# Two transformer blocks on cached keys and values: sums over the partitions as bf16 pairs, an earlier mean, a reordered end, and longer DRAM rows

## The chip, the cores and the metric

The kernel runs on one core of one Trainium2 chip. The metric is the device time of one execution in microseconds (us). The profiles call the engines PE (matrix products; PEld is its weight loads), DVE and ACT (vector and scalar work), POOL, and SP, which issues the loads. PSUM is the memory, in banks, that PE writes its results to. The kernel before takes 2348.97 us (median of 3 runs, 2348.39 to 2350.38).

## The reference, cut to what matters

One decode step for 8 batch rows: attention (32 heads of 128, 4096 cached keys and values, its own cache for every row and head) and a feed-forward network (FFN), run twice with the same caches and weights. I call the two passes layer 0 and layer 1.

```python
def _layernorm(x, axis=-1, eps=1e-5):
    m = jnp.mean(x, axis=axis, keepdims=True)
    v = jnp.var(x, axis=axis, keepdims=True)
    return (x - m) / jnp.sqrt(v + eps)
# A_x [8,1,640]; A_k_cache, A_v_cache [8,32,4096,128]; wq [640,4096]; wo [4096,640]; w1 [640,1728]; w2 [1728,640]
# _A_ref: q = x @ wq; softmax(q k^T / sqrt(128)) v for each row and head; then @ wo
# _B_ref: relu(x @ w1) @ w2
    x = A_x
    x = x + _A_ref(_layernorm(x, axis=-1), A_k_cache, A_v_cache, A_wq, A_wo)
    x = x + _B_ref(_layernorm(x, axis=-1), B_w1, B_w2)
    x = x + _A_ref(_layernorm(x, axis=-1), A_k_cache, A_v_cache, A_wq, A_wo)
    x = x + _B_ref(_layernorm(x, axis=-1), B_w1, B_w2)
    return x
```

The caches are 537 MB, and on-chip memory can't hold them, so most of them are read twice, once for each layer (988 MB in all).

## The kernel before

The kernel visits head pairs one by one: layer 0 of one batch row, then layer 1 of the same row, with two visits of the next row's layer 0 in between. Keys and values come in tiles of 512 KB into a ring of 26 buffers (the tile `arena`). At the end of a row's layer 0 comes what I call a **turn**: the output projection (`wo`), the FFN, and the first queries of layer 1, each needing the one before. In a turn 21 of the 26 buffers keep tiles that layer 1 will use again, so only five buffers pass the stream on, one 512 KB load each. Three more tiles are put aside ("stash") in five PSUM banks and a small tile.

```python
G = 26          # buffers of 512 KB
SPARE = 5       # of these, free for the stream in a turn
STASH = 3
...
    first = [(which, hp, g) for which, hp in first for g in range(UNIT)]
    keep = set(first[: G - SPARE])
    stash = first[G - SPARE : G - SPARE + STASH]
```

The chain of a turn (and of the end of layer 1, which handles all 8 rows at once):

```python
        for k in range(n_up):
            c += [own(15, "up", k)]
            if k == min(1, n_up - 1):
                c += [own(0, "var"), own(0, "root")]
        c += [own(0, "relu")] + [own(14, "down", k) for k in range(n_down)] + [own(0, "add")]
        if layer == 0:
            c += [own(2, "mean"), own(0, "center")] + query(b, 0)
            c += [own(1, "var2"), own(0, "root2")] + query(b, 1)
```

Sums over the 128 partitions are matmuls with a matrix of ones, in fp32. In `do_w` the sum of the residual row is added to the sum of the last head pair's output, which four matmuls with the column sums of `wo` give ahead of time:

```python
        def var():
            nc.tensor.matmul(var_ps[:, :nb], lhsT=ones_f, rhs=st.pop("s2"), start=True, stop=True)
        def relu():                                    # relu and the norm's factor in one operation
                    nc.vector.scalar_tensor_tensor(
                        out=hT[:rows, fs], in0=h[:rows, fs], scalar=0.0,
                        in1=_free(st["rstd"][:rows], [(0, fs.stop - fs.start), (1, nb)]), op0=ALU.max, op1=ALU.mult,
                    )
        def mean():
            nc.tensor.matmul(mean_ps[:, :1], lhsT=ones_f, rhs=st.pop("s1"), start=True, stop=True)
...
    def do_w(i):
        ...                                            # 10 matmuls with wo
        if "sums" in st:
            st["sum"] = sum_ps[:, :nb]
            nc.tensor.matmul(st["sum"], lhsT=ones_f, rhs=st.pop("sums"), start=True, stop=False)
            for n in range(4):
                nc.tensor.matmul(st["sum"], lhsT=_free(wo_sum[...], [(0, P)]), rhs=..., start=False, stop=(n == 3))
```

The stash is copied back by two engines in turn, from one PSUM tile each:

```python
    stash = [ps.tile([P, 2 * BANK], BF16, name=f"stash{n}_ps") for n in range(STASH * per - 1)]
    stash.append(sm.tile([P, 2 * BANK], BF16, name="annex", bufs=1))
...
            copy = nc.vector.tensor_copy if n % 2 else nc.scalar.copy
            copy(out=arena[:, u * GW + n * 2 * BANK : u * GW + (n + 1) * 2 * BANK], in_=t)
```

In DRAM each of the 128 partitions has a row of 32 pieces of 8192 bf16 numbers (the keys or the values of a head pair): exactly 512 KiB.

## Time and profile before

| | before |
|---|---|
| time, median | 2348.97 us |
| DMA engines busy on the load queue | 99.2% of the span |
| bytes through that queue | 988.12 MB |
| PE busy | 1406.6 us, 60% |
| last cache tile landed (its semaphore, in the trace) | 2334.10 us |
| from there to the end | 13.9 us |
| 4 KiB packets slower than usual (over 164 ns, usual 159) | 1030 of 27904 |

From the page of the profile, lines of its parts 1, 2, 3 and 6. Part 2 has 40 equal slices of the span (59 us each); DMA is the busy share in tenths and GB/s what the engines moved.

```profile
span 2348.0 us, 42121 instructions
DMA  9999999999999999999999999999999999999997
GB/s 410 431 432 399 432 431 432 432 404 434 431 433 426 408 434 433 432 425 417 431 430 434 420 415 432 432 433 413 414 430 433 431 409 421 433 430 431 391 432 308
q1 hardware_dynamic: 75412, 988.12, 99.2%
arena<-in_A_kv_dram SPq DMA_DIRECT2D x218, 512.0 KB, 6.1
```

The engines are busy in every slice, but they don't move equally much. Slices at 431 to 434 GB/s are calm; the eight dips (399, 404, 408 and so on) are the eight turns. The slope from 4 KiB packets (159 ns) to 32 KiB packets (1213 ns) is 435 GB/s, which agrees with the ceiling of 435 GB/s that the Trainium skill gives (DMA: Bandwidth & Descriptors, "Where 436 GB/s comes from"). The same section says that loads from DRAM are held to a lower limit of about 358 GB/s; here they run at 431 to 434, so the measurement decides. So two things can be shortened: what comes after the last landing, and the turns. The last line is the view of loads: 218 loads of 512 KB, the size that the turns use, with a median of 6.1 us from issue to landing.

The windows view of before, one calm stretch and two in turns. Columns: stretch and its length in us, busy us (and count) of PE, PEld (the weight loads of PE), DVE, ACT and POOL, granted clock, DMA share, GB/s.

```profile
960.00:980.00 20.00, 10.62 (x108) 3.43 (x108) 3.58 (x14) 2.89 (x6) 0.39 (x2) 0.50 1.01 433
1640.00:1660.00 20.00, 15.76 (x296) 10.33 (x291) 4.00 (x23) 4.23 (x16) 2.54 (x12) 0.50 1.00 368
2200.00:2220.00 20.00, 17.03 (x356) 11.19 (x357) 5.53 (x27) 6.17 (x18) 2.54 (x12) 0.50 0.93 360
```

The timeline of before, a part of the turn at 1644 us, with lines left out (start, length, engine, line, operation, out<-in, count, and in brackets the idle time before it and what ended it):

```profile
1644.38 0.60 PE L527 MATMUL small_ps<-hT,w_sb 128*128 128x1 bf16 x14 [0.32 <-DVE lsum L721]
1644.91 0.60 PE L621 MATMUL o_ps<-arena,P_sb 128*4 128x512 bf16 x4
1645.44 0.59 PE L540 MATMUL small_ps<-s_16759,few 128*128 128x1 f32 x2
1646.06 0.17 DVE L544 SCALAR_TENSOR_TENSOR xc<-small_ps,xT 128x5 f32<-128x5 f32 x1 [0.69 <-PE small_ps L540]
1646.28 0.25 PE L734 MATMUL small_ps<-few,o_sb 100*128 100x2 bf16 x4 [0.25 <-DVE xc L544]
1646.45 0.60 PE L621 MATMUL o_ps<-arena,P_sb 128*4 128x512 bf16 x4
1646.61 0.15 DVE L744 TENSOR_TENSOR oT<-small_ps,invL 128x2 bf16<-128x2 f32 x1
1647.66 0.41 PE L751 MATMUL small_ps<-oT,wo_sb 128*128 128x1 bf16 x10 [0.25 <-ACT qo L605]
1647.99 0.60 PE L621 MATMUL o_ps<-arena,P_sb 128*4 128x512 bf16 x4
1648.52 0.59 PE L507 MATMUL small_ps<-s_16773,few 128*128 128x1 f32 x2
1649.04 0.59 PE L621 MATMUL o_ps<-arena,P_sb 128*4 128x512 bf16 x4
```

L527 is the last part of the FFN's second product ("down"), L540 the fp32 mean (two instructions, 0.59 us), L507 the fp32 sum of squares for the queries, L621 are value tiles of the stream, L734 and L751 belong to the next row's attention output. A buffer comes free with each L621; they start at 1644.91, 1646.45, 1647.99 and 1649.04.

The timeline of before, the end, with lines left out:

```profile
2335.62 0.27 PE L734 MATMUL small_ps<-few,o_sb 100*128 100x2 bf16 x4 [0.75 <-ACT o_sb L729]
2336.14 0.41 PE L751 MATMUL small_ps<-qo,wo_sb 128*128 128x8 bf16 x10 [0.25 <-DVE qo L744]
2336.41 0.57 PE L757 MATMUL small_ps<-arena,few 128*128 128x8 f32 x2
2337.94 0.95 PE L501 MATMUL small_ps<-arena,w_sb 128*128 128x8 bf16 x30 [0.85 <-DVE xT L485]
2339.68 1.44 PE L501 MATMUL small_ps<-arena,w_sb 128*128 128x8 bf16 x40 [0.36 <-ACT arena L435]
2341.82 2.92 PE L527 MATMUL small_ps<-arena,w_sb 128*128 128x8 bf16 x70 [0.71 <-DVE arena L520]
2345.03 0.29 PE L782 MATMUL small_ps<-ident,ends 128*40 128x128 bf16 x1 [0.29 <-DVE ends L534]
```

The last value matmul ends at 2334.87 us. From it to the `wo` product (L751, "W") 1.27 us pass, from W to "up" (L501) 1.80, from up's start to down's end (L527) 6.80, and from there to the output's matmul (L782) 0.29.

### The profile page before, as it was taken

How to read it: one execution, taken by the hardware profiler on the slowest of the kernel's cores; microseconds unless marked ns; L12 is line 12 of the kernel's file. 1: busy time of each engine (PE TensorE's matmuls, PEld its weight loads, DVE VectorE, ACT ScalarE, POOL GpSimd, SP SyncE). 2: the span in 40 equal slices, each digit the busy share in tenths (PEclk: the TensorE clock that was granted, in tenths of full speed). 3: DMA queues.
4: the chain of work that ended last, by engine and by line, in shares of the span. 5: the costliest groups of instructions: out<-in, count | busy, mean ns of one | idle time of the engine just before them, and what ended most of it. 6: DMA issues, size and time to landing. Idle time of an engine off the chain costs nothing.

```text
span 2348.0 us, 42121 instructions
## 1 busy us (share of the span) xinstructions
PE 1406.6 (60%) x18352; PEld 593.5 (25%) x18352; DVE 477.1 (20%) x1928; ACT 430.0 (18%) x995; POOL 59.5 (3%) x296
## 2 busy tenths in 40 slices
PE   3547655585555855558545685556754577545856
PEld 1214211151112511125111341113311133111523
DVE  1113211121112211122111221112211122112212
ACT  1111211121111221112111121111211112111211
POOL 0000000000000000000000000000000000000000
PEclk9999955555555555555555555555555555555555
DMA  9999999999999999999999999999999999999997
GB/s 410 431 432 399 432 431 432 432 404 434 431 433 426 408 434 433 432 425 417 431 430 434 420 415 432 432 433 413 414 430 433 431 409 421 433 430 431 391 432 308
DMA packets 75597, 990.81 MB, mean 422 GB/s; under 512 B 8468, under 2 KB 8468, under 8 KB 36372
## 3 DMA queue, kind: packets, MB, share of 16 engines
q1 hardware_dynamic: 75412, 988.12, 99.2%
q8 instruction: 143, 2.34, 0.4%
q14 instruction: 42, 0.34, 0.0%
HBM read 988.08 MB, written 0.01 MB: 421 GB/s over the span
## 4 chain that ended last, share of the span: by engine, by line
DMA 70%; PE 20%; ACT 5%; DVE 3%; issue 1%; SPq 0%; DVEq 0%; ACTq 0%; POOL 0%; POOLq 0%
DMA arena<-in_A_kv_dram 70%; PE o_ps L621 5%; PE s_ps L639 4%; PE s_ps L629 4%; ACT P_row L689 2%; PE small_ps L597 1%; ACT P_sb L695 1%; ACT o_sb L729 1%; PE small_ps L734 1%; DVE mrow L647 1%; PE small_ps L501 1%; PE small_ps L702 1%; PE small_ps L751 1%; ACT nmax L687 1%; ACT nmax L691 1%
## 5 line engine op out<-in xcount | busy, mean ns | idle before, releaser
L621 PE MATMUL o_ps<-arena,P_sb 128*4 128x512 bf16 x4096 | 597.3, 595 | 420.4 <-DMA arena<-in_A_kv_dram 418.1
L629 PE MATMUL s_ps<-arena,qz 128*4 128x512 bf16 x3040 | 408.4, 598 | 259.6 <-DMA arena<-in_A_kv_dram 248.9
L621 PEld LDWEIGHTS <-P_sb 128*4 128x4 bf16 x4096 | 111.4, 88 | 548.8 <-issue 532.6
L647 DVE TENSOR_REDUCE mrow<-s_ps 100x1 bf16<-100x512 f32 x190 | 131.9, 694 | 355.2 <-PE s_ps L629 355.2
L729 ACT CAST o_sb<-o_ps 100x512 bf16<-100x512 f32 x256 | 150.0, 586 | 272.7 <-PE o_ps L621 270.7
L687 ACT ACTIVATE nmax<-small_ps 100x1 f32<-100x1 f32 x106 | 18.1, 171 | 800.8 <-PE small_ps L676 800.8
L639 PE MATMUL s_ps<-qo,arena 128*128 128x1 bf16 x4224 | 141.1, 165 | 33.0 <-DMA arena<-in_A_kv_dram 16.4
L639 PEld LDWEIGHTS <-arena 128*128 128x128 bf16 x4224 | 130.0, 104 | 45.4 <-DMA arena<-in_A_kv_dram 27.7
L629 PEld LDWEIGHTS <-qz 128*4 128x4 bf16 x3040 | 61.9, 84 | 309.2 <-issue 291.2
L709 DVE CAST P_sb<-small_ps 128x64 bf16<-128x64 f32 x190 | 42.6, 224 | 474.4 <-PE small_ps L702 474.4
L702 PE MATMUL small_ps<-few,P_row 100*128 100x16 bf16 x760 | 52.4, 179 | 96.8 <-ACT P_row L689 96.8
L687 ACT ACTIVATE nmax<-small_ps,q_scale 100x1 f32<-100x1 f32 x84 | 22.0, 261 | 418.5 <-PE small_ps L676 418.5
L721 DVE TENSOR_REDUCE lsum<-small_ps 128x2 f32<-128x64 f32 x256 | 57.4, 224 | 168.4 <-PE small_ps L715 168.4
L661 DVE TENSOR_REDUCE diag<-small_ps 1x2 bf16<-1x16 f32 x190 | 30.8, 162 | 280.6 <-PE small_ps L654 273.5
L702 PEld LDWEIGHTS <-P_row 100*128 100x128 bf16 x760 | 35.1, 107 | 191.7 <-ACT P_row L689 186.9
L734 PEld LDWEIGHTS <-o_sb 100*128 100x128 bf16 x1024 | 49.6, 108 | 108.7 <-ACT o_sb L729 77.4
L734 PE MATMUL small_ps<-few,o_sb 100*128 100x2 bf16 x1024 | 67.4, 170 | 11.4 <-DVE xc L544 1.8
L689 ACT ACTIVATE P_row<-s_ps,nmax 100x512 bf16<-100x512 f32 x106 | 72.8, 687 | 3.4
L597 PE MATMUL small_ps<-xq,wq_sb 128*128 128x1 bf16 x1280 | 52.0, 165 | 32.1 <-DVE qo L744 26.3
L654 PE MATMUL small_ps<-few,mrow 100*1 100x16 bf16 x190 | 35.7, 188 | 55.3 <-DVE mrow L647 55.3
L689 ACT ACTIVATE P_row<-s_ps,nmax,q_scale 100x512 bf16<-100x512 f32 x84 | 65.4, 778 | 2.8
L597 PEld LDWEIGHTS <-wq_sb 128*128 128x128 bf16 x1280 | 52.8, 104 | 45.3 <-issue 44.5
(205 smaller groups left out, 859.7 us busy)
## 6 DMA issues: line engine op xcount, KB each, us to landing
arena<-in_A_kv_dram SPq DMA_DIRECT2D x126, 4096.0 KB, 23.1
arena<-in_A_kv_dram SPq DMA_DIRECT2D x89, 2048.0 KB, 21.2
arena<-in_A_kv_dram SPq DMA_DIRECT2D x218, 512.0 KB, 6.1
arena<-in_A_kv_dram SPq DMA_DIRECT2D x16, 3072.0 KB, 22.0
arena<-in_A_kv_dram SPq DMA_DIRECT2D x38, 1024.0 KB, 10.4
arena<-in_A_kv_dram SPq DMA_DIRECT2D x10, 2560.0 KB, 19.9
arena<-in_A_kv_dram SPq DMA_DIRECT2D x15, 1536.0 KB, 20.4
wq_sb<-in_A_wq_dram SPq DMA_DIRECT2D x4, 1280.0 KB, 17.7
```

Of the source, the lines that this page charges most:

```text
L597: nc.tensor.matmul(q_ps[:, h : h + 1], lhsT=wq_sb[:, g, c, (2 * n + h) * Dh : (2 * n + h + 1) * Dh], rhs=xlns[b][:, 0, c : c + 1], start=( ...
L621: nc.tensor.matmul(o_ps[32 * c : 32 * c + CJ, :], lhsT=P_tiles[i][:, h, j : j + CJ], rhs=arena[:, at + c * CJ * Dh : at + (c + 1) * CJ * D ...
L629: nc.tensor.matmul(s_ps[32 * c : 32 * c + CJ, :], lhsT=qz[:, i % 3, c // 2, 3 - g : 3 - g + CJ], rhs=arena[:, at + c * BANK : at + (c + 1) ...
L639: nc.tensor.matmul(s_tiles[i][:, j : j + 1], lhsT=arena[:, at + n * P : at + (n + 1) * P], rhs=qo[:, b, h : h + 1], start=True, stop=True,)
L647: nc.vector.tensor_reduce(out=m_tiles[i][:OR, :1], in_=s_ps[:OR], axis=AX.X, op=ALU.max)
L687: nc.scalar.activation(out=nm[:OR, :1], in_=max_ps[:OR, :1], func=ACT.Copy, scale=less)
L689: nc.scalar.activation(out=P_rows[i][:OR], in_=s_ps[:OR], func=ACT.Exp, bias=nm[:OR, :1], scale=more)
L702: nc.tensor.matmul(P_ps[:, k * 4 * CJ : (k + 1) * 4 * CJ], lhsT=P_row[:OR, k * P : (k + 1) * P], rhs=rsel[:OR], start=True, stop=True,)
L709: nc.vector.tensor_copy(out=P_tiles[i].rearrange("p h (c k) -> p h c k", k=BANK // P), in_=P_ps.rearrange("p (k h c) -> p h c k", k=BANK / ...
L721: nc.vector.tensor_reduce(out=L, in_=lsum_ps.rearrange("p (h j) -> p h j", h=2), axis=AX.X, op=ALU.add)
L729: nc.scalar.copy(out=o_tiles[i][:OR], in_=o_ps[:OR, :].rearrange("p (j d) -> p j d", j=CJ))
L734: nc.tensor.matmul(oy[i][:, :2], lhsT=o_tiles[i][:OR, j, :], rhs=gsel[:OR, j, :], start=(j == 0), stop=(j == CJ - 1))
```

## The change

The change wants to shorten the turns and the end.

- **Longer rows:** each partition's DRAM row gets 4 KiB more, so that the rows don't start 512 KiB apart.
- **The layer-0 part (turns):** each fp32 sum becomes two bf16 matmuls (the rounded value and the rest, made by two DVE operations). The mean of the residual row is taken off one visit earlier. The norm's factor is multiplied in after the FFN instead of at the relu.
- **The end part:** the same for layer 1; besides, the four value tiles of the last head pair are used as weights, so that their result needs no gathering; the sum comes before W; the FFN runs in pieces, with up in two PSUM banks by turns and down in five. For that, the five stash tiles become one tile, and the temporaries of the start and the end move from a buffer of the ring to the small stash tile (`annex`).

The diff, cut to its core:

```diff
+PAD = 2048
...
+        if layer:
+            for k in range(n_up):
+                c += [own(15, "down", k)] + [own(0, "var"), own(0, "root")] * (k == n_up // 2)
+            return c + [own(0, "add")]
...
             if last_of[layer, b] == i and (layer == 0 or b == B - 1):
-                chains[-1] += [(0, ("S", i)), (16, ("W", i)), (0, ("YC", i))] + finish(layer, b)
+                chains[-1] += [(14, ("W", i)), (0, ("YC", i))] + finish(layer, b)
             elif layer == 0 or b == B - 1:
                 chains[-1] += [(10, ("W", i)), (0, ("Y", i))]
+                if last_of[layer, b] == next(v for v in range(i + 1, NV) if visits[v][:2] == (layer, b)):
+                    chains[-1] += [(0, ("S", i)), (2, ("SM", i)), (0, ("SC", i))]
...
-    stash = [ps.tile([P, 2 * BANK], BF16, name=f"stash{n}_ps") for n in range(STASH * per - 1)]
+    stash_ps = ps.tile([P, (STASH * per - 1) * 2 * BANK], BF16, name="stash_ps")
+    stash = [stash_ps[:, n * 2 * BANK : (n + 1) * 2 * BANK] for n in range(STASH * per - 1)] + [annex]
...
+    def halves(s, name):
+        t = temp([P, s.shape[1], 2], BF16, name)
+        nc.vector.tensor_copy(out=t[:, :, 0], in_=s)
+        nc.vector.tensor_tensor(out=t[:, :, 1], in0=s, in1=t[:, :, 0], op=ALU.subtract)
+        return t
+
+    def over_partitions(out, t):
+        for k in range(2):
+            nc.tensor.matmul(out, lhsT=ones_p, rhs=t[:, :, k], start=(k == 0), stop=(k == 1))
...
         def var():
-            nc.tensor.matmul(var_ps[:, :nb], lhsT=ones_f, rhs=st.pop("s2"), start=True, stop=True)
+            over_partitions(var_ps[:, :nb], st.pop("s2"))
...
+                for n in range(CJ) if i == len(visits) - 1 else ():   # last V tile as weights
+                    nc.tensor.matmul(
+                        (s_ps if h else o_ps)[:, :1], lhsT=arena[:, at + (c * CJ + n) * Dh : at + (c * CJ + n + 1) * Dh],
+                        rhs=P_tiles[i][:, h, j + n : j + n + 1], start=(j + n == 0), stop=(j + n == NJ - 1),
+                    )
...
-    kv = kv.reshape(B, p, -1)
+    kv = np.pad(kv.reshape(B, p, -1), ((0, 0), (0, 0), (0, PAD)))
```

## The prediction

> **What bounds it now.** DMA. The page has the 16 DMA engines 99.2% busy on the load queue and 988 MB in 2348.0 us. Steady stretches of the windows view run at 424 to 441 GB/s. By the DMA packets of the trace, a 32 KiB packet takes 1213 ns and a 4 KiB one 159 ns, as do 90% of each size; the slope is 435 GB/s, the fabric ceiling that the Trainium skill gives (DMA: Bandwidth & Descriptors, "Where 436 GB/s comes from"). What can move:
>
> 1. The tail. The last load's wait ends at 2331.8 us (timeline), 16.3 us before the end.
> 2. Eight turns from layer 0 to layer 1, one for each batch row: windows there show 360 to 415 GB/s and PE 80 to 88% busy. 21 of 26 buffers are kept there, the rest filled by 512 KB loads (218, landing after 6.1 us), and buffers come free only as PE's chain moves. Packets over their minimum sum to 20 us of DMA time, some 15 in the turns. In the worst stretch (1646 to 1655 us, about 310 GB/s) PE takes some 1.5 us per tile against 1.25 for a load: I read this as underfed DMA.
>
> **Costs of the change.**
> - Partition sums: an fp32 matmul takes 0.56 to 0.59 us; two bf16 ones should take about 0.15 (four of the same form take 0.26). Three or four per turn: 1.2 to 1.7 us less PE. Each adds two DVE operations of 0.15 us.
> - Norm factor behind the FFN: relu waited for PE, not for the factor: about 0.
> - In a turn's first half this falls into slack (tiles land 1.24 us apart); in the second, PE-paced, it saves about 0.6 us. Turns: 8 x 0.6, say 4.5 us in all (0 to 10).
> - Last V tile as weights: 64 weight loads at 31 ns are 2.0 us, as long as the 16 wide matmuls; but the 0.59 us cast and the four gathering matmuls go: from the end of V to W 1.27 us becomes about 0.5, saves 0.8.
> - Sum before W, the mean already off, and up starting in another bank: from W to up 1.8 us becomes 1.0, saves 0.8.
> - Last FFN in pieces: from up's start to down's end 6.8 us becomes about 5.6; one more DVE operation (0.2) at the end. Saves 1.0; tail together 2.5.
> - Longer rows: the same page ("Latency and other measured facts") reports 207 against 214 GB/s for a 512 KiB row pitch, which this kernel has. Here packets are at their minimum outside the turns, and well-fed 4 KiB packets too (412 GB/s at 1636 us), so I expect about 1 us; if the slow packets of the turns are HBM conflicts instead of underfeeding, up to 12.
>
> **Prediction.** 2349 - 2.5 - 4.5 - 1 = 2341 us, 8 in 10 between 2330 and 2346. Faster by over 2%: 0.02; within 2%: 0.97; slower: 0.01.
>
> **Right or wrong.** From the last load's wait to the end: 13.8 us instead of 16.3. Steady windows at 431 GB/s; turn windows up by some 10 GB/s, not to 430. 4 KiB packets: slow ones fewer by a third, minimum still 159 ns.
>
> **What would make it wrong.** Slow packets vanishing in the turns with PE's pace unchanged: then it was the row pitch, and the time is nearer 2330. Or the added DVE steps cost what PE saves; then only the tail gains.

## More of the kernel before

All engines run a list of operations in a fixed order that `plan` makes. Pieces of the turn's chain are put between the matmuls of tiles, so each engine's order is fixed too.

In the turns the DMA share still reads 1.00 at 368 GB/s. A "busy" engine there holds packets that take longer than their usual time; a share alone wouldn't show it.

## The result

| | time, median (lowest to highest) | ratio to before, with 95% interval |
|---|---|---|
| before, same rounds | 2349.58 us (2348.39 to 2351.96), 6 runs | |
| after | 2346.44 us (2344.99 to 2347.91), 6 runs | 0.9985 (0.9972 to 0.9998) |

A ratio is the mean time of one kernel's fast runs over the mean of the other's in the same rounds, so it is not quite the ratio of the medians. The change gains about 3 us of the 8 that were predicted. Two later measurements of the same kernel are told below: 0.9989 both times.

Lines of the page of after (parts 1, 2 and 3):

```profile
span 2343.2 us, 42314 instructions
GB/s 411 430 432 402 431 431 432 431 407 435 430 431 428 412 434 433 432 426 409 431 435 430 423 409 436 429 432 415 416 434 431 432 410 424 431 431 431 393 433 330
q1 hardware_dynamic: 75412, 988.12, 99.4%
```

The dips stand where they stood. Most are one to four GB/s higher, but two are lower (417 to 409 and 415 to 409). The windows view of after:

```profile
960.00:980.00 20.00, 10.62 (x108) 3.42 (x108) 3.58 (x14) 2.89 (x6) 0.39 (x2) 0.50 1.00 430
1640.00:1660.00 20.00, 15.81 (x314) 10.52 (x311) 5.00 (x30) 4.76 (x16) 2.54 (x12) 0.50 1.00 384
2200.00:2220.00 20.00, 16.81 (x386) 11.08 (x384) 4.72 (x22) 7.05 (x19) 2.54 (x12) 0.50 0.97 377
```

These two turn windows gained 16 and 17 GB/s. That looks like the predicted success, but a window at a fixed time holds another piece of the work in each kernel. To compare equal work, I cut the load stream of each trace at the same byte counts, into eight stretches around the turns and the calm ones between, and added up the time. The stretches of the turns took 510.0 us before and 507.8 after; the calm ones 1816.0 and 1816.5. In all the traces the calm stretches sum to 1815.7 to 1817.7 us. (The cuts weren't kept. With new ones, at the bytes landed 32 us before and after `xq` of each turn in the trace of before, the turns take 511.6 and 509.6 us, and the rest up to the last landing 1822.5 in both and 1821.2 to 1824.3 in all traces.) So nearly every difference between two runs is in the turns or behind the last landing. The turns of three profiled runs of the kernel after took 507.8, 509.4 and 515.2 us: one profile can't settle a question of 3 us here.

The end of after, in the timeline, with lines left out (compare the lines of before):

```profile
2332.46 0.37 PE L487 MATMUL small_ps<-annex,few 128*128 128x8 bf16 x2 [0.31 <-DVE annex L481]
2332.69 0.36 PE L672 MATMUL o_ps<-P_sb,arena 128*128 128x1 bf16 x8
2332.91 0.35 PE L672 MATMUL s_ps<-P_sb,arena 128*128 128x1 bf16 x8
2333.51 0.26 PE L829 MATMUL s_ps<-qo,wo_sum 128*128 128x8 bf16 x4 [0.25 <-DVE qo L803]
2334.36 0.55 PE L544 MATMUL s_ps<-annex,w_sb 128*128 128x8 bf16 x15 [0.32 <-DVE annex L521]
2337.11 1.37 PE L572 MATMUL stash_ps<-annex,w_sb 128*128 128x8 bf16 x45
2338.38 0.91 PE L572 MATMUL stash_ps<-annex,w_sb 128*128 128x8 bf16 x25
2339.82 0.30 PE L852 MATMUL small_ps<-ident,ends 128*40 128x128 bf16 x1 [0.53 <-DVE ends L587]
```

| piece of the end, us | before | after | saved | predicted |
|---|---|---|---|---|
| last landing to the end of the last V matmul | 0.77 | 1.11 | -0.34 | - |
| V's end to W (in after to the sum, L829, which stands first) | 1.27 | 0.25 | 1.02 | 0.8 |
| W (in after the sum) to up | 1.80 | 0.85 | 0.95 | 0.8 |
| up's start to down's end | 6.80 | 4.93 | 1.87 | 1.2 |
| down's end to the output's matmul | 0.29 | 0.53 | -0.24 | -0.2 |
| the output's matmul to the end of the span | 2.95 | 3.39 | -0.44 | - |
| last landing to the end | 13.88 | 11.06 | 2.82 | 2.5 |

The end does what was expected. Two losses hadn't been foreseen. The last part of V had landed at 2332.15 us and starts at 2332.69, because the mean's matmul (L487, first line) stands before it in PE's order and waits 0.31 us for DVE to make the two halves (the rounded value and the rest). And the last piece, with the output's store in it, is 0.3 to 0.45 us longer in every profiled kernel that has the end part, and also in `one_stash`, which hasn't; why, I didn't try.

The same part of a turn as above, after, with lines left out:

```profile
1643.46 0.60 PE L572 MATMUL small_ps<-hT,w_sb 128*128 128x1 bf16 x14 [0.31 <-DVE lsum L779]
1643.99 0.60 PE L679 MATMUL o_ps<-arena,P_sb 128*4 128x512 bf16 x4
1644.63 0.16 DVE L481 CAST s1h<-s_16854 128x1 bf16<-128x1 f32 x1
1644.84 0.36 PE L487 MATMUL small_ps<-s1h,few 128*128 128x1 bf16 x2 [0.25 <-DVE s1h L481]
1645.23 0.17 DVE L594 SCALAR_TENSOR_TENSOR xc<-small_ps,xT 128x5 f32<-128x5 f32 x1 [0.25 <-PE small_ps L487]
1645.45 0.24 PE L792 MATMUL small_ps<-few,o_sb 100*128 100x2 bf16 x4 [0.26 <-DVE xc L594]
1645.63 0.60 PE L679 MATMUL o_ps<-arena,P_sb 128*4 128x512 bf16 x4
1645.90 0.16 DVE L481 CAST s2h<-s_16872 128x1 bf16<-128x1 f32 x1
1646.09 0.16 DVE L482 TENSOR_TENSOR s2h<-s_16872,s2h 128x1 bf16<-128x1 f32 x1
1646.17 0.15 DVE L807 TENSOR_TENSOR oT<-small_ps,invL 128x2 bf16<-128x2 f32 x1
1647.03 0.41 PE L816 MATMUL small_ps<-oT,wo_sb 128*128 128x1 bf16 x10 [0.25 <-ACT qo L655]
1647.36 0.60 PE L679 MATMUL o_ps<-arena,P_sb 128*4 128x512 bf16 x4
1647.89 0.21 PE L487 MATMUL small_ps<-s2h,few 128*128 128x1 bf16 x2
1648.03 0.60 PE L679 MATMUL o_ps<-arena,P_sb 128*4 128x512 bf16 x4
```

This is the step that failed, to be seen in one place. Count from the start of the last down matmul. The mean's matmul is shorter (0.36 instead of 0.59 us). But it now waits for a cast on DVE (0.25), and the add before it, which carries the norm's factor, takes 0.22 us instead of 0.16 (L580, L534 of before); so xc starts 1.77 us after down instead of 1.68. Then the two DVE operations of the second pair of halves stand before the operation `oT` in DVE's order: oT starts 2.71 us after down instead of 2.23. The next two value tiles start 2.17 and 3.90 us after down instead of 2.07 and 3.61: PE has less to do, and these buffers come free *later*. Only the second sum, 0.21 us instead of 0.59, brings the time back: the third tile starts 4.57 us after down instead of 4.66. Of the 0.6 us that were predicted for this half of a turn, 0.1 is left here.

### The profile page after: what moved, and what is told of

Read it like the earlier page. It is cut to its first block, busy times and chain, and to the rows that moved or that the text cites. A ratio compares the mean times of both kernels' runs of the same rounds, so it can differ in the third digit from the quotient of the medians.

```text
span 2343.2 us, 42314 instructions
## 1 busy us (share of the span) xinstructions
PE 1401.7 (60%) x18396; PEld 583.6 (25%) x18396; DVE 495.1 (21%) x2014; ACT 430.1 (18%) x994; POOL 59.6 (3%) x296
## 4 chain that ended last, share of the span: by engine, by line
DMA 70%; PE 18%; ACT 6%; DVE 4%; issue 2%; SPq 0%; DVEq 0%; ACTq 0%; POOL 0%; POOLq 0%
DMA arena<-in_A_kv_dram 70%; PE o_ps L679 5%; PE s_ps L687 4%; PE s_ps L697 3%; ACT P_row L747 2%; PE small_ps L647 1%; ACT o_sb L787 1%; DVE mrow L705 1%; ACT P_sb L753 1%; PE small_ps L792 1%; ACT arena L626 1%; PE small_ps L760 1%; PE small_ps L816 1%; ACT nmax L745 1%; DVE hmx L724 0%
## 6 DMA issues: line engine op xcount, KB each, us to landing
arena<-in_A_kv_dram SPq DMA_DIRECT2D x38, 1024.0 KB, 10.6
```

## The experiments

**How parts were told apart.** I wrote one kernel with three switches (longer rows, layer-0 part, end part). With all three on, its instructions stand in the same order on each engine as those of after; with all off, as those of before. My first theory was the prediction's: in a turn PE paces the stream, and less work on PE gives time. Rivals: PE's work lies in slack, and the new order costs as much as it saves; the merged stash tile delays the turns; the longer rows do it all.

### First call: each part alone, and far less PE work

`tail_only`, the end part alone:

```diff
+PAD = 0
+TURN = False
+TAIL = True
```

> The kernel before, with only the end changed (last V tile as weights, early mean of the last attention output, last FFN in pieces, temporaries in their own tile); layer 0 and the row pitch as before. Theory A (each part works as I predicted, the turn's gain of 4.5 us was merely hidden in noise): about 2.8 us faster than before, and the turn part alone a further 4.5 us. Theory B (the turns give nothing): the end is the whole gain, 2.8 us here, the same as the whole change. In the profile both want 11.0 to 11.2 us from the last landing to the end of the span, against 13.9 before.

Measured: 2349.53 us (2345.87 to 2350.45), ratio 0.9991 (0.9977 to 1.0005). The trace shows 11.0 us after the last landing, so the end part does its 2.8 us there; the total gains about 2.

`turn_only`, the layer-0 part alone (`PAD = 0`, `TURN = True`, `TAIL = False`):

> The kernel before, with only the layer-0 part of the change (partition sums as two bf16 parts, early mean, norm factor behind the FFN), end and row pitch as before. Theory A: 4.5 us faster than before, DMA time of packets over their minimum falls from 20 us to about 15. Theory B: within 1 us of before, and that sum stays at 19 to 20 us.

Measured: 2354.21 us (2350.47 to 2355.70), ratio 1.0013 (1.0001 to 1.0026). The part that was to save 4.5 us *costs* 3 (0 to 6 by the interval).

`pad_only`, the longer rows alone:

```diff
+PAD = 2048
-    W = A_kv.shape[2] // (2 * NP)
+    W = (A_kv.shape[2] - PAD) // (2 * NP)
-    kv = kv.reshape(B, p, -1)
+    kv = np.pad(kv.reshape(B, p, -1), ((0, 0), (0, 0), (0, PAD)))
```

> The kernel before with rows 4 KiB longer and nothing else. If the slow 4 KiB packets of the turns are HBM conflicts of the 512 KiB pitch: their number falls well below the 1030 of before and the time falls by up to 12 us. If they are DMA waiting for free buffers: 1000 to 1060 slow packets, time within 1 us of before.

Measured: 2350.09 us (2346.88 to 2352.47), ratio 0.9996 (0.9984 to 1.0009). Not told apart from nothing by itself.

`light_turn`, wrong (relative error 0.835): the kernel before, with 14 of 70 up matmuls and 5 of 70 down matmuls in layer 0 (the edit without its `stop` flags).

```diff
-                for c in range(DC):
+                for c in range(DC if layer else 1):
...
-            for f, fs in enumerate(f_sizes):
+            for f, fs in enumerate(f_sizes if layer else f_sizes[:1]):
```

> The kernel before, wrong on purpose: the layer-0 FFN keeps 14 of its 70 up matmuls and 5 of its 70 down matmuls, so PE has some 4.5 us less to do in each of the eight turns; order, waits and loads are unchanged. If PE's work paces the turns (theory A), DMA time over the packets' minimum falls from 20 us to under 10 and the time falls by 8 us or more. If the turns are paced by something else (the round trip of loads through the five free buffers, or chains of waits between engines), the time falls by under 3 us and that sum stays near 20 us.

Measured: 2345.97 us (2343.11 to 2347.78), ratio 0.9980 (0.9968 to 0.9993). The pages have PE busy for 1406.6 us before and 1383.2 us here, 23 us less (the 36 us of the expectation were an estimate that the page doesn't bear out), and only 4.7 us come back. PE's waits for loads around the turns rose by about as much (33 to 55 us, from 30 us before each `xq` to 35 us after it). So the FFN's work on PE is mostly *not* what paces a turn: take it away, and PE waits for tiles. That is against my prediction's picture.

### Second call: combinations, and one more buffer

`after_again` is the kernel after, unchanged.

> The whole change once more, so that its parts are compared on one chip. As measured before: about 3 us faster than the kernel before. If the turn part costs 3 us and the end gives 2.8, as the parts alone suggest, then about 0 to 1 us faster, unless the longer rows give something beside the turn part.

Measured: 2346.19 us (2344.97 to 2350.52), ratio 0.9989 (0.9976 to 1.0002).

`after_nopad`, the kernel after with `PAD = 0`:

> The whole change with rows of the old length. If the row pitch matters only beside the turn part (interaction): about 4 us slower than the whole change, and slow 4 KiB packets near the 1192 of the turn part alone against 1029. If the pitch does nothing: same as the whole change within 1.5 us, and 950 to 1200 slow packets whichever the pitch is.

Measured: 2351.31 us (2348.06 to 2353.88), ratio 1.0003 (0.9989 to 1.0017). In the same call the whole change gained 2.6 us by its ratio, so without the longer rows it loses all of it: by the ratios, the longer rows are worth 0.0014 x 2350 = 3.3 us there.

`turn_pad`, the layer-0 part with longer rows:

> The layer-0 part together with longer rows, end as before. If the pitch matters beside the turn part: about 1 us slower to 1 us faster than the kernel before, against 3 us slower for the turn part alone. If the pitch does nothing: 2 to 4 us slower, as the turn part alone was.

Measured: 2348.51 us (2347.13 to 2352.61), ratio 0.9997 (0.9984 to 1.0009), about the same as the longer rows alone.

`g27`, wrong (relative error 0.745): the kernel before with one more buffer for the stream. Room for it comes from leaving four of the 14 blocks of `w2` out, so 0.66 MB (about 1.5 us at 431 GB/s) aren't loaded.

```diff
-G = 26
-SPARE = 5
+G = 27
+SPARE = 6
-    w2_sb = wres.tile([P, FC, D], BF16, name="w2_sb")
+    w2_sb = wres.tile([P, FC - 4, D], BF16, name="w2_sb")
-                    y[:, c, :], lhsT=w2_sb[:fs, f, c * P : (c + 1) * P], rhs=st["hT"][:fs, f, :],
+                    y[:, c, :], lhsT=w2_sb[:fs, f % (FC - 4), c * P : (c + 1) * P], rhs=st["hT"][:fs, f, :],
```

> The kernel before with one more buffer, 27 in place of 26, so that six and not five are free in a turn; the 4 KiB for it are taken from the second FFN weights, of which four of 14 row blocks are replaced by others (wrong on purpose; 0.66 MB less to load, worth 1.5 us). PE's work is unchanged. If the round trip of loads through the free buffers paces the turns: DMA time over the packets' minimum falls from 20 us to under 12 and the time by 8 us or more. If PE's work paces them: the time falls by 1.5 to 4 us and that sum stays at 17 us or more.

Measured: 2339.66 us (2338.87 to 2340.47), ratio 0.9956 (0.9943 to 0.9968). One buffer more is worth 10.3 us by the ratio, some 9 without the smaller load, with PE doing the same work. The stretches of the turns fall from 510.0 to 500.4 us. This is by far the largest lever found. I read it so: in a turn the stream lives on the round trip of five buffers (freed by PE, issued, landed after 5 to 6 us, used, freed), and a sixth hides more of it. With right results it doesn't fit: the build fails, with nearly 4 KiB for each partition missing.

### Third call: more PE work, and versions without the layer-0 part

`double_sums`: longer rows, and every fp32 sum of layer 0 done twice (one of the three places):

```diff
-            nc.tensor.matmul(var_ps[:, :nb], lhsT=ones_f, rhs=st.pop("s2"), start=True, stop=True)
+            s2 = st.pop("s2")
+            for n in range(2 - layer):
+                nc.tensor.matmul(var_ps[:, :nb], lhsT=ones_f, rhs=s2, start=True, stop=True)
```

> The kernel before with longer rows, and each of the four fp32 partition sums of a turn done twice (the result is the same), so that PE has 4 x 0.57 = 2.3 us more to do in each turn, just where the change takes 1.2 to 1.7 us away. If PE's pace in the turns counts as I predicted (0.6 us gained for 1.2 to 1.7 us less work): 7 us slower than the longer rows alone, and the eight turns together 515 us or more by the landed bytes, against 508.8. If PE's work there is mostly covered by waits for loads: within 3 us, turns 507 to 512.

Measured: 2360.31 us (2358.86 to 2361.76), ratio 1.0039 (1.0026 to 1.0051). Against `pad_only` that is 0.0043 x 2350 = 10 us more. By the pages PE is busy for 11 us more (1409.1 to 1420.1; the expectation had 18, but two sums in a row take 1.0 us and not twice 0.59). So PE time *at these places of the chain* does count, nearly in full, while the FFN's matmuls in `light_turn` counted at a fifth (4.7 of 23). The fp32 sums weren't worthless to remove; something ate what their removal gave.

`light_pad`, wrong as `light_turn`, with longer rows:

> The light turn (wrong on purpose, 4.5 us less PE work in each turn) with longer rows. If 36 us less PE work give only about 5 us, as with the old rows: 5 us faster than the longer rows alone, turns at 502 to 505 us against 508.8; PE waits for loads in the turns up from 55 us to over 70. If the old pitch had hidden a gain: 10 us faster or more, turns under 499.

Measured: 2343.41 us (2342.14 to 2344.69), ratio 0.9968 (0.9955 to 0.9980), 2.8 us less than `light_turn` by the ratios: again about 3 us for the longer rows.

`tail_pad`: end part and longer rows, without the layer-0 part (`PAD = 2048`, `TURN = False`, `TAIL = True`):

> The whole change without its layer-0 part: end and longer rows. If the layer-0 part is worth nothing with longer rows: the same as the whole change, 3 us faster than before, turns at 507 to 510 us. If it is worth what I predicted: 4.5 us slower than the whole change.

Measured: 2345.32 us (2344.19 to 2347.67), ratio 0.9976 (0.9963 to 0.9989). That is below the whole change's 0.9985 and 0.9989, though the intervals overlap.

`sm_late`: the kernel after, with layer 1's mean matmul moved behind the last value tile.

```diff
-                chains[-1] += [(14, ("W", i)), (0, ("YC", i))] + finish(layer, b)
+                chains[-1] += [(2, ("SM", i)), (0, ("SC", i))] * layer + [(14, ("W", i)), (0, ("YC", i))] + finish(layer, b)
...
-                    chains[-1] += [(0, ("S", i)), (2, ("SM", i)), (0, ("SC", i))]
+                    chains[-1] += [(0, ("S", i))] + [(2, ("SM", i)), (0, ("SC", i))] * (1 - layer)
```

> The whole change, with the mean's two matmuls of the last attention output moved behind the last V tile: in the trace of the change they make PE wait 0.5 us for DVE in front of the last V part. Expected: 0.4 to 0.5 us less from the last landing to the end (11.06 us before, to about 10.6), the rest unchanged; by time not to be told from the whole change.

Measured: 2349.82 us (2345.86 to 2351.11), ratio 0.9988 (0.9974 to 1.0002). The end took 10.6 us instead of 11.06, but other kernels with the mean where it was also show 10.6, one of them with a granted clock of 1.0 there. The 0.5 us that the mean's matmul delays the last tile aren't shown to be won back. Inconclusive.

### Fourth call: the stash, the sums, the sum of all findings

What was open by then: where the saved PE time of the layer-0 part went. A suspect in the trace was the merged stash tile. Timeline of `pad_only`, two copies back from the stash:

```profile
1666.00 1.02 ACT L577 COPY arena<-stash_ps 128x1024 bf16<-128x1024 bf16 x1
1666.16 0.69 DVE L577 COPY arena<-stash_ps 128x1024 bf16<-128x1024 bf16 x1
```

`one_stash` is `pad_only` with the stash in one tile:

```diff
-    stash = [ps.tile([P, 2 * BANK], BF16, name=f"stash{n}_ps") for n in range(STASH * per - 1)]
+    stash_ps = ps.tile([P, (STASH * per - 1) * 2 * BANK], BF16, name="stash_ps")
+    stash = [stash_ps[:, n * 2 * BANK : (n + 1) * 2 * BANK] for n in range(STASH * per - 1)]
```

> The kernel before with longer rows, and the five PSUM tiles of stashed keys and values made one tile of the same size; no other difference. If the merge is what makes ACT's and DVE's copies back follow each other: they don't overlap here either, and the two attention outputs after them come 0.9 and 0.7 us later in each turn (6.4 and 5.9 us apart instead of 5.5 and 5.2). If that chain is on the critical path: 5 us or more slower than the longer rows alone; if DMA is full there anyway: 0 to 3 us slower.

The same two copies in the timeline of `one_stash`:

```profile
1666.77 1.02 ACT L578 COPY arena<-stash_ps 128x1024 bf16<-128x1024 bf16 x1
1667.82 0.69 DVE L578 COPY arena<-stash_ps 128x1024 bf16<-128x1024 bf16 x1 [0.83 <-ACT arena L578]
```

The DVE copy now waits 0.83 us for ACT's, though each reads its own bank. Two attention outputs in each turn come later for it (6.4 and 5.9 us after the one before instead of 5.5 and 5.2, as in the kernel after). Measured time: 2348.63 us (2347.63 to 2350.44), ratio 0.9989 (0.9976 to 1.0001): no worse than `pad_only`.

`split_stash` is the reverse, the kernel after with the stash in five tiles again (cut; the scaling at the end then takes five DVE operations instead of one):

```diff
-    stash_ps = ps.tile([P, (STASH * per - 1) * 2 * BANK], BF16, name="stash_ps")
-    stash = [stash_ps[:, n * 2 * BANK : (n + 1) * 2 * BANK] for n in range(STASH * per - 1)] + [annex]
+    stash = [ps.tile([P, 2 * BANK], BF16, name=f"stash{n}_ps") for n in range(STASH * per - 1)] + [annex]
...
-            y = stash_ps.bitcast(FP32).rearrange("p (c n) -> p c n", n=BANK)[:, :DC, :nb]
+            y = [t.bitcast(FP32)[:, :nb] for t in stash[:DC]]
```

> The whole change, but the five stash tiles stay apart; the last FFN sums into the five of them and is scaled by five small DVE operations instead of one, which costs 0.5 to 0.8 us at the end. If the merge costs nothing: 0.5 to 0.8 us slower than the whole change. If it costs 2 to 5 us: 1.5 to 4 us faster than the whole change, and the spacing of the two outputs is back at 5.5 and 5.2 us.

Measured: 2347.22 us (2345.89 to 2351.28), ratio 0.9985 (0.9973 to 0.9998), the ratio of the kernel after. So a delay of some 1.6 us in each turn, plain in the timeline, costs nothing that shows: on the critical path it would be 13 us in eight turns. And `turn_only`, which has the five tiles apart, lost 3 us, while `tail_pad`, which has them merged, is among the fastest. This theory fell.

`sums_only`: longer rows, and the bf16 pairs in layer 0, without the early mean and with the factor at the relu.

> The kernel before with longer rows and only the partition sums of layer 0 as two bf16 parts; mean and norm factor stay where they were. If the cheaper sums are worth what the doubled ones cost (9 us for 2.3 us per turn, so about 5 us for 1.2 to 1.7): 4 to 6 us faster than the longer rows alone, and from the last output to the query scale 0.6 us or more less than 23.1 us. If the added DVE steps eat it: within 1.5 us, and 22.8 to 23.2 us.

Measured: 2348.41 us (2346.63 to 2350.78), ratio 0.9988 (0.9975 to 1.0000). Within the noise of `pad_only` (0.9996) and `one_stash` (0.9989): the bf16 pairs by themselves neither help nor hurt by more than the noise.

`best`: end part, longer rows, turns as before, the stash in five tiles, layer 1's mean late.

> End part and longer rows, the turns as in the kernel before, stash tiles apart, the last mean behind the last V tile. If the turn part and the merge both cost: 6 to 9 us faster than the kernel before, and 3 us or more faster than the whole change. If only noise separated them: 3 to 5 us faster than before.

Measured: 2347.22 us (2344.05 to 2348.78), ratio 0.9977 (0.9963 to 0.9990). That is the same as `tail_pad`; the last two edits add nothing that shows.

### Fifth call: the whole change against the version without the layer-0 part

`after_third` is the kernel after, unchanged, and `tail_pad_again` is `tail_pad`, on one chip in the same rounds.

> The whole change, beside the kernel without its layer-0 part on the same chip. As before: ratio to the kernel before 0.9985 to 0.9989, about 3 us faster.

Measured: 2348.88 us (2345.10 to 2353.47), ratio 0.9989 (0.9975 to 1.0003).

> End part and longer rows without the layer-0 part, same chip. If the layer-0 part costs 2 us: ratio near 0.9976 as in its first run, and 2 to 3 us faster than the whole change. If it gives and costs nothing: the same as the whole change within 1 us, ratio 0.998 to 0.999. If it gained what I predicted: 4.5 us slower than the whole change, ratio above 1.

Measured: 2346.69 us (2343.95 to 2347.88), ratio 0.9978 (0.9965 to 0.9990). The version without the layer-0 part is again the faster one, by 2.6 us by the ratios, again with overlapping intervals.

### What the parts are worth together

Ten of these ratios are of kernels that differ only in the three switches:

| kernel | longer rows | layer-0 part | end part | ratio |
|---|---|---|---|---|
| pad_only | x | | | 0.9996 |
| turn_only | | x | | 1.0013 |
| tail_only | | | x | 0.9991 |
| turn_pad | x | x | | 0.9997 |
| tail_pad, tail_pad_again | x | | x | 0.9976, 0.9978 |
| after_nopad | | x | x | 1.0003 |
| after, after_again, after_third | x | x | x | 0.9985, 0.9989, 0.9989 |

If the parts add up, the least-squares values (ratios times 2350 us) are -2.6 us for the longer rows, +2.5 us for the layer-0 part and -2.5 us for the end part, each with a standard error of about 0.5 us from the scatter of the ten results about this sum (0.9 us); from the intervals of the single ratios it would be about 0.9. The intervals of single kernels (about 3 us to each side) are wider than the parts, and the pairs differ: with longer rows and without the end part, the layer-0 part cost 0.2 us (`turn_pad` against `pad_only`), in the three other pairings 2.5 to 3.1. So the signs rest on the ten results together. The traces leave it open whether the parts add up: with the new cuts, the layer-0 part lengthens the turns by about 5 us with old rows (511.6 to 516.9 and 513.5 to 518.1), and by nothing clear with longer rows (510.6 to 510.0; 512.1 and 511.3 to 509.6, 510.4 and 517.0). The granted clock is no rival: it ranges from 0.55 to 1.0 in the timed runs, and within the runs of a kernel the time changes with it by -0.6 us per unit, with a standard error of 1.7.

### Where the layer-0 part lost it

I followed the chain of the eight turns by the starts of its operations: O2 and O1 are the last two attention outputs of layer 0, xf the FFN's input, then relu, xq (the centred input of the next queries), O, the next row's output that follows, and K, the first key tile of the row's layer 1. The second sum of the query's norm, which the change shortens too, lies between O and K. Means over eight turns, us:

| kernel | O2 to O1 | O1 to xf | xf to relu | relu to xq | xq to O | O2 to O | O to K | O2 to K |
|---|---|---|---|---|---|---|---|---|
| before | 3.48 | 2.04 | 6.48 | 7.95 | 0.61 | 20.57 | 2.70 | 23.27 |
| pad_only | 3.49 | 2.05 | 6.50 | 8.03 | 0.61 | 20.68 | 2.68 | 23.36 |
| sums_only | 3.51 | 1.70 | 6.77 | 8.06 | 0.91 | 20.94 | 2.23 | 23.18 |
| turn_pad | 3.70 | 1.57 | 6.78 | 8.16 | 0.91 | 21.12 | 2.20 | 23.32 |
| turn_only | 3.71 | 1.54 | 6.84 | 8.30 | 0.91 | 21.29 | 2.24 | 23.53 |
| after | 3.70 | 1.54 | 6.83 | 7.95 | 0.91 | 20.92 | 2.26 | 23.18 |
| double_sums | 3.49 | 2.47 | 6.81 | 8.16 | 0.67 | 21.59 | 2.96 | 24.56 |

The fp32 sum after W is gone, and O1 to xf is 0.5 us shorter. But then:

- xf to relu is 0.3 us longer. PE waits there for tiles that land no earlier: 0.8 us in each turn in `after`, `turn_pad` and `turn_only`, none in `before`. That is slack, as predicted for a turn's first half.
- O2 to O1 is 0.2 us longer in the kernels with the early mean (not in `sums_only`): its matmuls now stand in that visit and wait for DVE's halves.
- xq to O is 0.3 us longer in all kernels with the pairs: the two DVE operations of the second pair stand before O in DVE's order.
- relu to xq, where the fp32 mean was, is no shorter.
- O to K is 0.4 to 0.5 us shorter: the second sum is the cheaper pair, and this makes up for what was lost before O.

Up to O the layer-0 part costs 0.2 to 0.7 us in each turn, but at K nearly all of it is made up: from O2 to K `turn_pad` takes 23.32 us against 23.36 in `pad_only`, `turn_only` 23.53 against 23.27 in `before`, and the three traces of the kernel after 23.18 to 23.39 against 23.47 and 23.52 in those of `tail_pad`. So the chain is neither shorter nor longer by more than some 0.3 us, where the prediction had it 0.6 shorter. For `double_sums` against `pad_only` the chain to K gives 8 x 1.20 = 9.6 us and the ratio 10.

So what is shown is that the layer-0 part as a whole doesn't gain (+2.5 us in the ten ratios; no shorter chain in the traces), that the merged stash isn't the reason, and that the pairs alone cost at most little. Why it should *cost* 2.5 us isn't shown: the chain to K accounts for almost none of it. The order of the operations on DVE, the early mean and the norm's factor weren't changed by themselves in an experiment; that the early mean's wait, the casts and the DVE order eat what the cheaper sums give is what the traces suggest.

## Why the prediction was right or wrong

- **Bound by DMA, with turns and end as the only places to gain: right.** The calm stretches took 1816.0 and 1816.5 us before and after.
- **The end, 2.5 us: right.** 2.8 us by the trace (13.88 to 11.06), 2.5 by the ratios. The text of the prediction has the wrong start, 2331.8 us: the wait it read was of a weight load; the last tile landed at 2334.10. So "13.8 instead of 16.3" is off at both ends by 2.4 to 2.7 us, and its difference holds. The FFN in pieces saved 1.87 us instead of 1.2, and two unforeseen losses (0.34 and 0.44) took the surplus.
- **The turns, "in the second, PE-paced, it saves about 0.6 us. Turns: 8 x 0.6, say 4.5 us in all": wrong, and this is the step that failed.** The runs show a cost of about 2.5 us in its place (by the ten ratios together; `turn_only` alone 1.0013), 7 us away from the predicted gain. Two things were wrong in it. First, PE's busy time was taken for pace: 80 to 88% busy looked like a limit, but `light_turn` took 23 us away and got 4.7, while one buffer more gave 10.3 without touching PE's work. Second, where PE's time does count (`double_sums`: 10 us for 11 of added work), the chain of a turn didn't get shorter: from O2 to K it takes 23.32 us in `turn_pad` against 23.36 in `pad_only`, in place of 0.6 less. The prediction lists the two DVE operations for each sum, but its 0.6 us shows no term for them; each sum now waits for the first of them, and what stands behind both in DVE's order waits as well. Why the sign turned, and not only the gain went, stays open. In the turn shown the pair of the mean took 0.36 us, with a wait for the second half in it; at the end of the same trace, where nothing waits, a pair took 0.19, near the 0.15 of the prediction. The prediction named this as its last way to be wrong ("the added DVE steps cost what PE saves; then only the tail gains"), and gave it no weight in the sum.
- **The norm's factor behind the FFN, about 0:** not tried alone. Relu waited for PE before, and xf to relu became no shorter. The add that now carries the factor took 0.22 us instead of 0.16 in the turn shown.
- **The longer rows, about 1 us: too small; about 2.6 was found.** Packets outside the turns are at 159 and 1213 ns with and without, as predicted. The Trainium skill (DMA: Bandwidth & Descriptors, "Latency and other measured facts") gives 207 GB/s for copies at a row pitch of 512 KiB, against 214, its full rate, at a padded pitch, which is 3%; in calm stretches no such loss is to be seen here. Which step of a turn the longer rows shorten isn't shown. A 512 KB load that is issued with at most two others in flight lands a little sooner on average: 5.56 to 5.86 us in the five traces with the old rows (mean 5.72), 5.36 to 5.76 in fourteen with longer rows (mean 5.57; `g27`, with its sixth buffer, left out). The ranges overlap, with some 20 such loads in most traces, so this is a hint and no cause.
- **"Slow ones fewer by a third": wrong.** 1030 before, 1029 after. Nor is their number a good gauge: it is 914, 1029 and 1187 in three runs of the same kernel.
- **Turn windows up by 10 GB/s:** two shown windows rose by 16 and 17, and still only 2 us were won in the turns of that trace. Windows at fixed times were a poor test.

The version to take is `tail_pad`: longer rows and the end part, the turns as they were. It ran at 0.9976 and 0.9978 of before, about 5.4 us faster than before and, by the ratios, 2.5 us faster than the whole change.

## What to carry to other kernels

A busy engine in a stretch isn't yet the one that paces it: double its work and take it away before you cost a saving there, for the two needn't be worth the same (here the doubled sums came through nearly in full, the cut FFN at a fifth). When a slow step is traded for a shorter one with helpers on another engine, cost the whole chain, look at what stands behind the helpers in that engine's fixed order, and follow the chain to a point behind the last step that changed: ended one step too soon, it showed a loss here that the next step made up for. Compare stretches of equal bytes, not of equal times, and measure the parts of a change one by one: here two parts of 2.5 us gained, and the third gave as much back.

## What the Trainium skill lacked or had wrong

- DMA: Bandwidth & Descriptors, "Latency and other measured facts", gives the effect of a row pitch of 512 KiB as a rate of copies between DRAM tensors (207 against 214 GB/s). For loads into on-chip memory the usual packet is no slower here (4 KiB 159 ns, 32 KiB 1213 ns with both pitches); what longer rows shorten is the turns, by about 2.6 us of 2350, and how isn't shown. Whether the pitch alone does it wasn't tried with other sizes than 4 KiB.
- I found no page that gives the time from issue to landing of a 512 KB load into all 128 partitions that SyncE issues with few others in flight (there is a fit only for single loads that GpSimd issues). Here it is 5.4 to 5.9 us on average, where its bytes take 1.2 us at 431 GB/s. The size of the ring of buffers mattered most in this kernel (one buffer more in the turns: 10.3 us, 1.5 of it from a smaller load).
- Perfetto Trace Analysis, "Identifying the Most-Contended Engine", says to judge DMA by its throughput and not by its occupancy, because there are 16 engines. It doesn't say that an engine also reads as busy while its packets are slow: the profile has a DMA share of 1.00 at 368 GB/s in a turn and of 1.01 at 433 in a calm stretch.
- PSUM — Partial Sum Buffer, "PSUM bank collisions raise a hardware error", says that two engines run clean on different banks. Nothing here contradicts it: the two stash copies overlap when the banks belong to different tiles (1666.00 and 1666.16 us). But with the same banks in one tile the second copy waited 0.83 us for the first; the page doesn't say that the unit that a program waits for can be the tile rather than the bank.
